# The second half of batch 0: values mixed at full height and regrouped by transfers, keys two rows at a time, queries transposed for both quads

## The chip, the cores and the metric

The kernel runs on one NeuronCore of a Trainium2 chip. Five engines work from their own instruction queues: TensorE (PE, with weight loads shown apart as PEld), VectorE (DVE), ScalarE (ACT), GpSimd (POOL) and SyncE (SP). Instructions of one engine run in program order; engines wait for each other by semaphores. Transfers are issued by SP or POOL (one by ACT) and are carried out by 16 DMA engines. The metric is the device time of one execution in microseconds.

## The reference, cut to what matters

Two stages follow each other: a block-sorted attention and a mixture of four experts. q, k and v are 4 batches x 8 heads x 768 positions x 64; sort_net gives an 8 x 8 matrix per batch and head.

```python
for _ in range(5):                                   # P = sort_net, per batch and head
    P = exp(P - max); P /= rowsum; P /= colsum
k_sorted = einsum('bhij,bhjcd->bhicd', P, k_blocks)  # 8 blocks of 96 positions
v_sorted = einsum('bhij,bhjcd->bhicd', P, v_blocks)
attn = softmax(q_blocks @ k_sorted.T / 8)            # inside each block
x = (attn @ v_sorted)                                # 3072 tokens x 512
p = domain_probs / sum
out = sum_e p[:, e] * (relu(x @ w1[e]) @ w2[e])      # 512 -> 1024 -> 512, 4 experts
```

So each sorted block is a weighted sum of the 8 blocks of its head ("mixing"), and the attention is local to a block.

## The kernel before

**Names.** P = 128, NB = 8 blocks, CP = 16, R = 6, HB = 4 blocks (half of them), VW = 66. A quad (qd) is four heads; sg picks a pair of heads inside it and hh one of the pair. k and v of a quad lie in the tile `arena` with partition = (block j, c) and 6 rows of 64 per partition, so that a block's 96 positions are (c, r). A matmul with the matrix PI0 (built from the sorted weights and an identity mask) mixes the blocks.

**Batch 0 in halves.** Batch 0 has its own path (functions whose names begin with h_), worked in two halves of four output blocks (hf 0 and 1), and each half in two quarters of blocks (qq 0 to 3).

- `h_k` and `h_v` (lines 511 to 515) call `mix_half` (L485): 24 matmuls per quad (L495), each with one row r of one head as 128 x 64 weights and 64 moving columns, the two heads of a pair in the two halves of the output partitions. `mixed` (L503) copies the result from PSUM to `kTs[qd]` or `vT0[qd]`, both with head and dimension on the partitions.
- `h_w` (L517) transposes `vT0` back to position-major by 8 matmuls against the identity (L522), and copies to `vs0s[qd]` (L527), 96 partitions x (block, sg, hh, 66), whose two extra columns hold ones for the softmax sum.
- `h_q` (L264) transposes the queries in `q0` by 24 small matmuls per quad and half (L271) into `qT0[qd]`. q0 holds quad qd on the partitions 64 qd and up.
- `h_s` (L540) makes the scores of one quad and quarter and their exponentials (ACT, L556) in `ETs`; `h_a` (L561) multiplies them with `vs0s` (L567) and normalizes on DVE (L580, L581); `h_x` (L590) transposes into `xTs[0]` (L598, L602).
- `group0` (L666) and `second_layer0` (L708) are expert 0's two layers for batch 0, with matmuls at L679 and L714 and evacuations at L692 (ACT) and L723 (DVE). `own_weights` (L247) makes expert 0's token weights a column per token, by a transpose of `p_0` (6 x 128, f32).

**Order.** The order of all work is the order in which the program emits it; nothing is rearranged. Lines 1365 to 1417 are the first half by hand, with the keys' mixing of the second half (`h_k(0, 1)`, `h_k(1, 1)`) between the groups of the first layer. Then `h_v(0, 1)` and `h_q(0, 1)`, then `second_layer0(0, next_stages)`, which calls `next_stages` in the middle and at the end of each of its three column groups; every call takes the next entry of the list `later` (L1439). After six calls `chunk_first` for the experts 1 and 2 goes on taking entries (L790 matmuls, L796 evacuations on DVE).

**Buffers.** PSUM tiles come in turn from two pools of two buffers, `psA` (attention, function `psa`) and `psM` (experts, `psm`); a new tile waits until the one two before it has been read.

**Transfers.** SP issues, in order: two small loads at the start; then one step of `spread_weights` (L229): the store of the first token weights to DRAM (L241), the load of `p_0` (L242), the spread of four experts' token weights over 128 partitions, 512 KB (L217), and the store of the remaining token weights (L244); then `load_p_one` (L226), 128 KB, needed at L796 near 58.75 us. POOL issues the loads of q, k, v and of all expert weights (`load_w1` L131, `load_w2` L138).

Of the kernel before, what the change touches and what calls it, by code (L numbers as in the profile page):

```python
# [9 lines left out]
F32 = mybir.dt.float32  # L10
F16 = mybir.dt.float16
# [6 lines left out]
def kernel(  # L18
# [11 lines left out]
    nc = tc.nc  # L30
# [36 lines left out]
    def psa(shape, dtype, name):  # L67
        state["n"] += 1
        return psA.tile(shape, dtype, tag="ps", name=name)
# [53 lines left out]
    def head(b, nm, h):  # L123
        return natural[(b, nm, h // 4)][:, h % 4, :, :]
# [6 lines left out]
    def load_w1(e, parts=1):  # L131
        n = NKC // parts
        for i in range(parts):
            nc.gpsimd.dma_start(
                w1sb[e][:, ds(i * n, n)], moe_w1[e].rearrange("(kc p) f -> p kc f", p=P)[:, ds(i * n, n)]
            )
# [20 lines left out]
    def p_part(at, n):  # L157
        return Tt[2].rearrange("p a f x -> p (a f x)")[:, ds(2 * at, 2 * n)].bitcast(F32)
# [47 lines left out]

    p_dram = dramp.tile([E, N], F32, name="p_dram")
    p_sb = const.tile([P, R, 1], F32, name="p_sb")
    p_0 = p_part(2 * E * NT + NT, P)[0:R]
    ident6 = p_part(2 * E * NT + NT + P, R)[0:R]  # L210
    S_P = S // NT

    pbs = {}
# [15 lines left out]
    def spread_weights():  # L229

        nc.vector.tensor_reduce(p_den, p_in, AX.X, ALU.add)
        yield
        nc.vector.tensor_scalar(out=p_den, in0=p_den, scalar1=1e-9, scalar2=None, op0=ALU.add)
        yield
        nc.vector.reciprocal(p_den, p_den)
        yield
        nc.vector.tensor_tensor(
            p_out.rearrange("p e t -> p t e"), p_in, p_den.broadcast_to([P, NT, E]), ALU.mult
        )
        p_rows = p_dram.rearrange("e (p t) -> p e t", t=NT)  # L240
        nc.sync.dma_start(p_rows[0:S_P], p_out[0:S_P])  # L241
        nc.sync.dma_start(p_0, p_dram[0, 0:S].rearrange("(t p) -> t p", p=P))  # L242
        pbs[(0, 0)] = load_p(0, 0)
        nc.sync.dma_start(p_rows[S_P:P], p_out[S_P:P])  # L244
        yield

    def own_weights(ps):  # L247

        nc.tensor.transpose(ps, p_0, ident6)
        nc.vector.tensor_copy(p_sb.rearrange("p t o -> p (t o)"), ps)  # L250


# [11 lines left out]
    def h_q(qd, hf, copy):  # L264

        ps = psa([P, 2, R, 64], F16, f"ps_q_{qd}_{hf}")
        rows = ds(64 * qd, 64)
        for sg in range(2):
            for r in range(R):
                for hh in range(2):  # L270
                    nc.tensor.transpose(  # L271
                        ps[ds(D * hh, D), sg, r, :], q0[rows, hf, 2 * sg + hh, r, :], ident[rows, rows]
                    )
        copy(qT0[qd][:, :, hf], ps[:])
# [4 lines left out]
    sn16 = const.tile([GH, NB, NB, CP], F16, name="sn16")  # L279
    warm(84)  # L280
    p_steps = spread_weights()
    nc.gpsimd.tensor_copy(ident6, ident[0:R, 0:R])
    for it in range(5):
        nc.scalar.activation(sn[:], sn[:], AF.Exp, bias=0.0, scale=1.0)
        if it == 4:
# [199 lines left out]
    def mix_half(nm, qd, hf, pool, warm_up=0):  # L485

        ps = pool([P, 1024], F32, f"ps_m{nm}_{qd}_{hf}")
        keep_warm(ps[:, 0:P], warm_up)
        tails[(nm, qd, hf)] = ps[:, 2 * R * 64:1024].bitcast(F16).rearrange("p (n x) -> p n x", n=2)
        ps = ps[:, 0:2 * R * 64].rearrange("p (s r x) -> p s r x", s=2, r=R)  # L490
        for sg in range(2):
            for r in range(R):
                for hh in range(2):
                    h = 4 * qd + 2 * sg + hh
                    nc.tensor.matmul(  # L495
                        ps[ds(D * hh, D), sg, r, :],
                        head(0, nm, h)[:, r, :],
                        PI0[hf][:, h, :, :].rearrange("p i c -> p (i c)"),
                        start=True, stop=True,
                    )  # L500
        return ps

    def mixed(nm, qd, ps, i0, n, copy):  # L503

        dst = kTs[qd][:, 0:S] if nm == "k" else vT0[qd]
        copy(
            dst.rearrange("p (i x c) -> p x i c", i=HB, c=CP)[:, :, ds(i0, n)],
            ps.rearrange("p s r (i c) -> p (s r) i c", c=CP)[:, :, ds(i0, n)],
        )

    def h_k(qd, hf, copy, pool=psa):
        mixed("k", qd, mix_half("k", qd, hf, pool), 0, HB, copy)

    def h_v(qd, hf, copy, pool=psa):
        mixed("v", qd, mix_half("v", qd, hf, pool), 0, HB, copy)

    def h_w(qd, copy, i0=0, n=HB, at=None):  # L517

# [888 lines left out]
    h_x(1, act, [0], ps_s01)  # L1407
    evacuate00()
    group0(0, 1, 1, [2, 3])
    h_a(1, 1, ps_s11)  # L1410
    h_k(0, 1, act)
    group0(1, 1, 0, [0, 1])
    h_x(1, vec, [1], ps_s11)
    group0(1, 1, 1, [0, 1])
    h_k(1, 1, vec)
    group0(1, 1, 0, [2, 3])
    group0(1, 1, 1, [2, 3])


    load_w1(1)  # L1420
    load_w1(2)
    nc.gpsimd.memset(vo[:, :, :, ds(D, 2)], 1.0)
    nc.gpsimd.tensor_copy(
        maskv.rearrange("p (c i) -> p c i", i=NB),
        eye16.rearrange("p (c o) -> p c o", o=1).broadcast_to([P, CP, NB]),
# [2 lines left out]
    def builds(b):  # L1428
# [8 lines left out]
    builds(1)  # L1437

    later = [  # L1439
        [(h_q, 1, 1, vec)],  # L1440
        [(h_v, 1, 1, act)],
        [(h_s, 0, 2), (h_w, 1, vec)],
        [(h_w, 0, vec), (h_s, 1, 2)],
        [(h_a, 0, 2)],
        [(h_s, 0, 3), (h_a, 1, 2)],
        [(h_s, 1, 3), (h_a, 0, 3)],
# [6 lines left out]
            for f, *args in later.pop(0):  # L1453
                f(*args)

    h_v(0, 1, act)
    h_q(0, 1, vec)
    second_layer0(0, next_stages)
    load_queries(1, range(2))
    for qd in range(2):  # L1460
# [75 lines left out]
```

## Time and profile before

| what | us |
|---|---|
| median of 3 runs (359.15 to 359.76) | 359.17 |
| profiled execution: span from first to last instruction | 357.8 |
| median less span: what lies around the instructions | 1.4 |
| PE busy | 351.6 |
| DVE busy | 276.2 |
| ACT busy | 170.6 |
| POOL busy | 133.6 |
| first product of h_a with the second half, quad 0 / quad 1 | 35.91 / 37.39 |
| first L790 matmul | 37.65 |

The profiled execution is known by its span; its own total is not given apart from the runs. A line of the timeline has the start in us, the length in us, the engine, the source line, the operation, what it writes and reads, the shape, how often (x), and in brackets idle time before it with what ended it. Matmuls are pipelined, so the start-to-start distance of two pieces is their price, and the stated length includes the way through the array.

### The profile page before, as it was taken

What the parts mean: (1) busy time and instruction counts of PE and PEld (TensorE: products, weight loads), DVE (VectorE), ACT (ScalarE), POOL (GpSimd) and SP (SyncE); (2) the same over time, 40 slices, a digit from 0 to 9 for tenths busy, and PEclk for the clock granted to TensorE, in tenths of its full rate; (3) what the DMA queues carried; (4) which work ended last, traced back from release to release, by engine and by line L of the source; (5) the groups of instructions that cost most, each with busy time, mean ns of one, the idle gap of its engine ahead of it and who ended that gap; (6) DMA issues with size and microseconds to landing.
All of it is one profiled execution on the core that took longest, in us unless ns stands there. A gap on an engine that the chain in (4) does not pass through costs nothing.

```text
span 357.8 us, 9498 instructions
## 1 busy us (share of the span) xinstructions
PE 351.6 (98%) x3949; PEld 306.3 (86%) x3949; DVE 276.2 (77%) x552; ACT 170.6 (48%) x303; POOL 133.6 (37%) x149
## 2 busy tenths in 40 slices
PE   8899999999999999999999999999999999999996
PEld 8686867888888888888899988888888888888886
DVE  5754797869889587868978988896678886588963
ACT  2554240442434535367947258830288611688201
POOL 8864010375122222000535318840058800188400
PEclk9999999999999999999999999999999999999999
DMA  8999999999999999935996420005200015100011
GB/s 114 207 205 228 216 210 198 209 163 165 201 154 160 188 152 170 194 74 73 168 201 90 102 78 0 2 2 108 102 29 2 3 39 138 61 0 2 2 73 46
DMA packets 72022, 40.51 MB, mean 113 GB/s; under 512 B 40614, under 2 KB 66732, under 8 KB 71980
## 3 DMA queue, kind: packets, MB, share of 16 engines
q0 software_dynamic: 36576, 19.93, 41.9%
q1 hardware_dynamic: 35260, 19.92, 28.5%
q8 instruction: 31, 0.51, 0.6%
q14 instruction: 11, 0.09, 0.1%
q10 hardware_dynamic: 144, 0.07, 0.1%
HBM read 42.13 MB, written 6.34 MB: 135 GB/s over the span
## 4 chain that ended last, share of the span: by engine, by line
PE 95%; DVE 2%; ACT 1%; DMA 0%; issue 0%; DVEq 0%
PE ps_h L790 18%; PE ps_Q L1264 18%; PE ps_p L774 12%; PE ps_X L1121 10%; PE ps_Z L1121 7%; PE ps_Q L1121 7%; PE ps_Z L1264 6%; PE ps_h L679 3%; PE ps_o L714 3%; PE ps_p L830 3%; PE ps_a L453 2%; PE ps_s L418 2%; PE ps_k L399 1%; PE ps_v L365 1%; PE ps_a L567 1%; PE ps_mk L495 1%
## 5 line engine op out<-in xcount | busy, mean ns | idle before, releaser
L790 PE MATMUL ps_h<-xT,w 128*128 128x256 f16 x576 | 67.5, 273 | 0.0
L790 PEld LDWEIGHTS <-w 128*128 128x128 f16 x576 | 55.2, 98 | 7.2
L796 DVE SCALAR_TENSOR_TENSOR Hb<-ps_h,pb 128x1024 f16<-128x1024 f32 x34 | 41.5, 1223 | 17.2 <-PE ps_h L790 15.8
L1121 PEld LDWEIGHTS <-w 128*128 128x128 f16 x480 | 43.6, 98 | 4.8
L1134 POOL TENSOR_TENSOR arena<-tmp,pb 128x512 f16<-128x512 f32 x12 | 15.2, 1275 | 65.7 <-PE ps_Z L1121 49.8
L1264 PEld LDWEIGHTS <-Hb 128*128 128x128 f16 x320 | 31.1, 98 | 3.5
L1133 ACT ACTIVATE tmp<-tmp 128x512 f32<-128x512 f32 x46 | 29.0, 632 | 3.9 <-DVE tmp L1171 3.9
L1264 PEld LDWEIGHTS <-Sb 128*128 128x128 f16 x304 | 28.3, 98 | 3.0
L1121 PEld LDWEIGHTS <-arena 128*128 128x128 f16 x312 | 27.7, 98 | 2.9
L425 ACT ACTIVATE ET<-ps_s 96x768 f16<-96x768 f32 x24 | 18.0, 802 | 25.1 <-PE ps_s L418 24.8
L121 POOL DMA_DIRECT2D arena<-in_q_dram x24 | 19.9, 838 | 25.5 <-DMA q_ring<-arena 25.2
L408 ACT CAST kT<-ps_k 64x384 f16<-64x384 f32 x48 | 22.7, 473 | 13.3 <-PE ps_k L399 12.3
L1121 PE MATMUL ps_X<-ET,arena 128*128 128x256 f16 x168 | 25.2, 272 | 0.0
L1264 PE MATMUL ps_Q<-w,Hb 128*128 128x256 f16 x192 | 24.6, 273 | 0.0
L774 PEld LDWEIGHTS <-Hb 128*128 128x128 f16 x232 | 21.8, 98 | 3.0
L1127 DVE SCALAR_TENSOR_TENSOR Hb<-ps_X,pb 128x512 f16<-128x512 f32 x27 | 18.7, 691 | 7.0 <-PE ps_X L1121 7.0
L1141 ACT COPY ps_X<-ps_Z 128x512 f32<-128x512 f32 x27 | 15.4, 571 | 17.8 <-PE ps_Z L1121 17.8
L1121 PE MATMUL ps_Z<-xT,w 128*128 128x256 f16 (+1 forms) x176 | 22.5, 258 | 0.0
L760 DVE TENSOR_TENSOR Sb<-Hb 128x512 f16<-128x512 f16 x33 | 20.6, 647 | 0.0
L1148 ACT COPY tmp<-ps_X 128x512 f32<-128x512 f32 x26 | 15.2, 585 | 9.2 <-PE ps_X L1121 6.6
L1127 DVE SCALAR_TENSOR_TENSOR Hb<-ps_Z,pb 128x512 f16<-128x512 f32 x27 | 18.4, 682 | 1.3 <-PE ps_Z L1121 1.3
L1171 DVE TENSOR_TENSOR tmp<-ps_Q,tmp 128x512 f32<-128x512 f32 x26 | 17.8, 683 | 0.8 <-PE ps_Q L1121 0.8
(266 smaller groups left out, 741.6 us busy)
## 6 DMA issues: line engine op xcount, KB each, us to landing
w<-in_moe_w_dram POOLq DMA_DIRECT2D x6, 1024.0 KB, 27.9
pb<-p_dram SPq DMA_DIRECT2D x9, 512.0 KB, 7.0
arena<-in_k_dram POOLq DMA_DIRECT2D x8, 384.0 KB, 9.3
arena<-in_v_dram POOLq DMA_DIRECT2D x8, 384.0 KB, 7.5
vs<-arena SPq DMA_DIRECT2D x36, 66.0 KB, 4.9
arena<-in_q_dram POOLq DMA_DIRECT2D x24, 96.0 KB, 7.5
out_dram<-ob SPq DMA_DIRECT2D x9, 256.0 KB, 2.0
w<-in_moe_w_dram POOLq DMA_DIRECT2D x4, 512.0 KB, 12.5
```

What stands on the lines that cost most here:

```text
L121: nc.gpsimd.dma_start(t[:, h // 2, :, h % 2, :], q[b, h].rearrange("(t p) d -> p t d", p=P))
L408: nc.scalar.copy(kT[ds(D * hh, D), r], pk[ds(D * r, D), hh].rearrange("p a (i c) -> p a i c", c=CP),)
L425: nc.scalar.activation(ETs[2 * (pr % 2) + hh][:, 0:S].rearrange("c (a x) -> c a x", a=2), pss[hh][0:BLK, :, 0:HS], AF.Exp, bias=0.0, scale ...
L760: tt(sm[0], blk(0, 1), blk(1, 1), ALU.add)
L774: nc.tensor.matmul(ps, lhs(e, f), Ts[e][rhs][:, f, :], start=(first and e == es[0] and f == 0), stop=(done and e == es[-1] and f == KH - 1 ...
L790: nc.tensor.matmul(ps[:, f, :], w1sb[e][:, kc, ds((4 * g + f) * P, P)], xT[:, kc, ds(2 * c * P, 2 * P)], start=(kc == 0), stop=(kc == NKC ...
L796: nc.vector.scalar_tensor_tensor(out=Hb[:, homes.get(e, e), ds(4 * g, 4), :], in0=ps[:], scalar=0.0, op0=ALU.max, in1=weights(e).broadcast ...
L1121: nc.tensor.matmul(dst[:, ds(f * cols, cols)], a[lhs][:, k, ds((f0 + f) * P, P)], t[rhs][:, k, :], start=(first and f == 0 and k == 0), st ...
L1127: nc.vector.scalar_tensor_tensor(out=home(i, j), in0=src.rearrange("p (f x) -> p f x", f=m), scalar=0.0, op0=ALU.max, in1=weight(j).broadc ...
L1133: nc.scalar.activation(src, src, AF.Relu, bias=0.0, scale=1.0)
L1171: tt(t12, Q, u2, ALU.add)
L1264: nc.tensor.matmul(ps, lhs(e, f), Ts[e][rhs][:, f, part], start=(first and e == 0 and f == 0), stop=(e == E - 1 and f == KH - 1), skip_gro ...
```

## The change

The first half (hf 0) stays as it is. For the second half:

- **Values.** `h_v` and `h_w` go. `half_v(qd, sg)` uses PI0 as weights (128 x 64) and all six rows of a head as 384 moving columns, one matmul per head, so the result has (block, c) on 64 partitions. ACT copies it to `vo1s[qd]`, and after the second pair SP issues four transfers per quad, one per block, which move 16 partitions x 6 rows to 96 partitions of `vs0s[qd][:, i]`.
- **Keys.** `h_k` becomes `half_k`: two rows of a head as 128 x 128 weights, PI0 as 64 moving columns, 12 matmuls per quad; four copies per quad put it into `kTs[qd]`, two by ACT and two by DVE.
- **Queries.** `pair_q` copies the second half of q0 on DVE so that two heads lie side by side; `half_q` transposes both quads by 12 full transposes; two DVE copies fill `qT0`.
- **Token weights.** `p_0` becomes 128 x 128, zero but for six rows, and `own_weights` a plain f32 matmul.
- **Order.** The four half_v stand among the groups of the first layer where h_k was; half_k(0) precedes `second_layer0`; half_q and half_k(1) are the first two entries of `later`. The loads of w1 of the experts 1 and 2 are emitted earlier, with a fill for each vo1.

```diff
-    p_0 = p_part(2 * E * NT + NT, P)[0:R]
-    ident6 = p_part(2 * E * NT + NT + P, R)[0:R]
+    p_0 = p_part(2 * E * NT + NT, P)
+    ident6 = p_part(2 * E * NT + NT + P, R)
+    nc.gpsimd.memset(p_0, 0.0)
...
-        nc.sync.dma_start(p_0, p_dram[0, 0:S].rearrange("(t p) -> t p", p=P))
+        nc.sync.dma_start(p_0[0:R], p_dram[0, 0:S].rearrange("(t p) -> t p", p=P))
...
-        nc.tensor.transpose(ps, p_0, ident6)
+        nc.tensor.matmul(ps, p_0, ident6, start=True, stop=True)
...
-    nc.gpsimd.tensor_copy(ident6, ident[0:R, 0:R])
+    nc.gpsimd.tensor_copy(ident6, ident[:, 0:R])
...
+    vo1s = [vo, Tt[0].rearrange("p a f x -> p (a f x)")[:, 0:R * 4 * VW].rearrange("p (r h w) -> p r h w", r=R, h=4)]
+
+    def half_v(qd, sg, copy):
+
+        ps = psa([P, 2, 512], F32, f"ps_v0_{qd}_{sg}")[0:CP * HB]
+        for hh in range(2):
+            h = 2 * sg + hh
+            nc.tensor.matmul(
+                ps[:, hh, 0:R * D],
+                PI0[1][:, 4 * qd + h].rearrange("p i c -> p (i c)"),
+                head(0, "v", 4 * qd + h).rearrange("p r d -> p (r d)"),
+                start=True, stop=True,
+            )
+        vo1 = vo1s[qd][0:CP * HB]
+        copy(
+            vo1[:, :, ds(2 * sg, 2), 0:D],
+            ps[:, :, 0:R * D].rearrange("p h (r d) -> p r h d", r=R),
+        )
+        if sg:
+            for i in range(HB):
+                nc.sync.dma_start(
+                    vs0s[qd][:, i].rearrange("x s h w -> x (s h w)"),
+                    vo1[ds(i * CP, CP)].rearrange("c r h w -> c r (h w)"),
+                )
+
+    def half_k(qd, copies):
+
+        ps = psa([P, 2, 512], F32, f"ps_k0_{qd}")
+        pk = ps[:, :, 0:R * 64].rearrange("p h (s a i c) -> p h s a i c", s=2, i=HB, c=CP)
+        for hh in range(2):
+            for sg in range(2):
+                h = 4 * qd + 2 * sg + hh
+                for a in range(R // 2):
+                    nc.tensor.matmul(
+                        ps[:, hh, ds((sg * (R // 2) + a) * 64, 64)],
+                        head(0, "k", h)[:, ds(2 * a, 2), :].rearrange("p r d -> p (r d)"),
+                        PI0[1][:, h, :, :].rearrange("p i c -> p (i c)"),
+                        start=True, stop=True,
+                    )
+        kT = kTs[qd][:, 0:S].rearrange("p (i s c a r) -> p r s a i c", i=HB, s=2, c=CP, r=2)
+        for hh in range(2):
+            for r in range(2):
+                copies[hh](kT[ds(D * hh, D), r], pk[ds(D * r, D), hh])
+
+    q1 = Tt[1].rearrange("p a f x -> p (a f x)")[:, 0:2 * R * P].rearrange("p (s r x) -> p s r x", s=2, r=R)
+
+    def pair_q():
+
+        for sg in range(2):
+            nc.vector.tensor_copy(
+                q1[:, sg].rearrange("p r (h d) -> p r h d", h=2),
+                q0[:, 1, ds(2 * sg, 2)].rearrange("p h r d -> p r h d"),
+            )
+
+    def half_q(copy):
+
+        ps = psa([P, 2, 1024], F16, "ps_q1")
+        for sg in range(2):
+            for r in range(R):
+                nc.tensor.transpose(ps[:, sg, ds(r * P, P)], q1[:, sg, r], ident[:])
+        for qd in range(2):
+            copy(
+                qT0[qd][:, :, 1],
+                ps[:, :, 0:R * P].rearrange("p s (r q x) -> p s r q x", r=R, q=2)[:, :, :, qd],
+            )
...
     group0(0, 1, 1, [2, 3])
+    for vo1 in vo1s:
+        nc.gpsimd.memset(vo1[:, :, :, ds(D, 2)], 1.0)
+    load_w1(1)
+    load_w1(2)
     h_a(1, 1, ps_s11)
-    h_k(0, 1, act)
+    half_v(0, 0, act)
     group0(1, 1, 0, [0, 1])
     h_x(1, vec, [1], ps_s11)
     group0(1, 1, 1, [0, 1])
-    h_k(1, 1, vec)
+    half_v(0, 1, act)
+    pair_q()
     group0(1, 1, 0, [2, 3])
+    half_v(1, 0, act)
     group0(1, 1, 1, [2, 3])
-
-
-    load_w1(1)
-    load_w1(2)
-    nc.gpsimd.memset(vo[:, :, :, ds(D, 2)], 1.0)
+    half_v(1, 1, act)
...
     later = [
-        [(h_q, 1, 1, vec)],
-        [(h_v, 1, 1, act)],
-        [(h_s, 0, 2), (h_w, 1, vec)],
-        [(h_w, 0, vec), (h_s, 1, 2)],
+        [(half_q, vec)],
+        [(half_k, 1, (vec, act))],
+        [(h_s, 0, 2)],
+        [(h_s, 1, 2)],
         [(h_a, 0, 2)],
         [(h_s, 0, 3), (h_a, 1, 2)],
         [(h_s, 1, 3), (h_a, 0, 3)],
...
-    h_v(0, 1, act)
-    h_q(0, 1, vec)
+    half_k(0, (act, vec))
     second_layer0(0, next_stages)
```

## The prediction

> **What bounds the kernel now.** I read the page first: span, busy shares, and the chain that ended last.
>
> ```profile
> span 357.8 us, 9498 instructions
> PE 351.6 (98%) x3949; PEld 306.3 (86%) x3949; DVE 276.2 (77%) x552; ACT 170.6 (48%) x303; POOL 133.6 (37%) x149
> ...
> PE 95%; DVE 2%; ACT 1%; DMA 0%; issue 0%; DVEq 0%
> ```
>
> TensorE is busy for all but 6.2 us and makes up 95% of the chain, so any time it stands still is added to the end, and any matmul time saved is taken off it, unless a wait that follows takes it back. Of the waits of PE the longest two are 1.1 and 1.0 us, both before 12 us; after 28 us none is listed, so later slack can hardly give a delay back.
>
> Next, busy time by stretches: the changed stage runs from about 18 us to 37.65 us, where the first expert's matmuls (L790) begin.
>
> ```profile
> 18.20:28.04 9.84, 9.53 (x193) 8.55 (x190) 5.19 (x12) 5.99 (x10) 7.04 (x9) 1.00 1.24 206
> 28.04:37.65 9.61, 9.61 (x160) 5.64 (x155) 5.33 (x10) 3.71 (x6) 2.92 (x4) 1.00 1.13 229
> ```
>
> Columns after the length: PE, PEld, DVE, ACT, POOL busy, clock, share of the DMA engines, GB/s. PE is full; DVE and ACT have room; the DMA engines are over 1.1 busy, filled by the weight loads that POOL has queued. Then the timeline of PE, for the price of each piece and for when the attention products are wanted:
>
> ```profile
> 27.54 0.57 PE L495 MATMUL ps_mv<-Sb,arena 128*64 128x64 f16 x24
> 28.04 0.56 PE L271 MATMUL ps_q<-ident,T 64*64 64x64 f16 x24
> 28.54 1.04 PE L714 MATMUL ps_o<-w,Hb 128*128 128x512 f16 x4
> ...
> 35.91 0.41 PE L567 MATMUL ps_a<-Sb,ET 96*128 96x65 f16 x8
> ...
> 37.39 0.42 PE L567 MATMUL ps_a<-Sb,ET 96*128 96x65 f16 x8
> ```
>
> The prices are start to start: 24 small matmuls take 0.50. The L567 lines are h_a(0, 2) and h_a(1, 2), the first readers of the second half of the values. Last, the transfers that SP issues in this stretch, and the table of issues in the window 20 to 44 us (median time to landing last):
>
> ```profile
> 20.58 0.34 SPq L241 DMA_DIRECT2D p_dram<-T  x1
> 26.17 0.33 SPq L242 DMA_DIRECT2D T<-p_dram  x1
> 26.55 0.41 SPq L217 DMA_DIRECT2D pb<-p_dram  x1
> 27.00 0.49 SPq L244 DMA_DIRECT2D p_dram<-T  x1
> 27.62 0.53 SPq L226 DMA_DIRECT2D T<-p_dram  x1
> ```
>
> ```profile
> pb<-p_dram SPq DMA_DIRECT2D x1, 512.0 KB, 11.7
> ...
> T<-p_dram SPq DMA_DIRECT2D x1, 128.0 KB, 14.4
> p_dram<-T SPq DMA_DIRECT2D x1, 36.0 KB, 13.9
> ```
>
> The 36 KB of L244 land at 27.0 + 13.9 = 40.9 us, after the 512 KB of L217 (26.55 + 11.7 = 38.3) that were issued ahead of them on the same queue, and L226's 128 KB land after that, at 27.62 + 14.4 = 42.0. What SP issues here comes in order, and late.
>
> **The change part by part.**
>
> *PE, removed.* Four mixings of 24 matmuls (L495) at 0.50, two sets of 24 query transposes (L271) at 0.50, two sets of 8 value transposes (L522) at 0.48 and 0.54 (32.87 to 33.35, 34.22 to 34.76), and three gaps of 0.08 to 0.09 where PE goes from full tiles to half ones (25.53 to 25.61, 27.45 to 27.54, 29.41 to 29.50): 2.0 + 1.0 + 1.0 + 0.3 = 4.3 us.
>
> *PE, added.* half_v: 8 matmuls of 384 columns; two such (L365) take 65.05 to 65.37, so 0.16 each, 1.3. half_k: 24 matmuls with 128-column weights; six such (L399, twice as many columns) take 68.31 to 68.65, 0.057 each, 1.4; with half the columns it could be 0.03 each, 0.7. half_q: 12 transposes at 0.06 (L522), 0.7. own_weights: a full-height f32 matmul in place of the 6-row transpose, which takes 0.15; no row shows one, so 0.15 to 0.6. Sum 3.7 with 0.3 for it, so 0.6 saved, between 0.3 and 1.4.
>
> *PSUM and ACT.* psA has two buffers, and each half_v is emptied by ACT in 0.80 (L371), alternating with the 0.76 that each group evacuation takes. Replaying the order from L692's end at 24.61: the four copies end near 25.4, 26.9, 28.5 and 30.1. half_k(0) would be due at 28.0 but needs the buffer that is free at 28.5: 0.5 lost. half_q is due near 30.1 as the fourth copy ends: 0 to 0.1. Earlier, h_x(1) cannot start before the DVE product that ends at 24.62, and less stands in front of it: 0.15. These holds take 0.7, so h_a(0, 2) would be wanted at 35.91 - 0.6 + 0.7 = 36.0, between 35.2 and 36.4.
>
> *Other engines.* ACT gets 4 x 0.80 + 4 x 0.47 (L408) = 5.1 for 0.82 + 2 x 0.80 = 2.4. DVE gets pair_q (two copies of 768 f16, 0.42 to 0.56 each by L760 and L274), half_q's two at 0.56 and half_k's four at 0.56 (L602 on DVE) = 4.5 for 0.96 + 2 x 0.56 + 2 x 0.68 = 3.4. half_k writes with a step of several elements, which no row shows; if that doubled its copies, 1 us would be added on each engine and could reach PE at h_s. POOL gets small fills: p_0 in front of a wait of 1.22 us (L304), vo1 ahead of the two loads at L134 (some 0.3, with the load queue already full). I put all of this and the PE sum at nothing, because the wait below starts at 36.0 and hides whatever happens before it, up to 6 us.
>
> *The transfers, the added wait.* vs0s of the second half now arrives by eight transfers on SP: four per quad, each 96 pieces of 528 B, 51 KB. In SP's order they stand behind L241, L242, L217 and L244, all issued by one step of spread_weights. SP is free at 27.5, quad 0's values are copied at 26.9, and an issue takes 0.6 (L379), so quad 0 is issued from 27.5 to 29.9 and quad 1, copied at 30.1, from 30.1 to 32.5: long before L244 lands. They then move in order behind it. L226, now behind them, shows the pace: 128 pieces, 128 KB, in 1.1 us. A new transfer is 0.75 of that by pieces (0.83 us) and 0.40 by bytes (0.43); I take 0.65. h_a(0, 2) needs the first two: 40.9 + 1.3 = 42.2 (41.8 to 42.6). h_a(1, 2) needs the sixth: 40.9 + 3.9 = 44.8 (43.5 to 45.9).
>
> On PE, h_a(0, 2) waits from 36.0 to 42.2. Behind it stand in order four L714 (0.87), h_s(0, 3) and h_a(1, 2); these take 1.4 and then wait for 44.8. h_a(1, 2), at 37.39 before, starts at 44.9: 7.5 later (6.2 to 8.6). After it, the order is as before, and h_a(0, 3) and h_a(1, 3) find their data at 43.5 and 46.1, before they are due. L226 lands near 47, and its reader (L796) stood at 58.75. The loads of POOL yield some 2 us to 400 KB; the next values landed at 34.04 + 29.5 = 63.5, wanted at 64.94 plus the delay: covered.
>
> *The clock after the wait.* At its start PE is slow:
>
> ```profile
> 1.06:5.70 4.64, 4.64 (x44) 4.64 (x45) 2.31 (x11) 1.48 (x3) 4.35 (x8) 1.00 0.72 105
> 5.70:8.19 2.49, 2.49 (x44) 2.38 (x41) 1.89 (x11) 0.51 (x2) 2.41 (x5) 1.00 1.18 161
> ```
>
> 44 matmuls of 128 columns take 4.64 us, the next 44 take 2.49, although the clock column says 1.00 for both. No pause in this trace shows whether a stop of 6 us brings that back: between 0 and 4.64 - 2.49 = 2.2 us. I take 0.9: the slow stretch starts at 42.2, 2.6 us of it pass before h_a(1, 2), the remaining 2.0 lose nearly half.
>
> The Trainium skill, "TensorE: Matmul & The Clock Gate" (The HAM clock gate), says PE falls to half rate after an idle window of about 3.4 us and needs about as long to come back; that would make the loss 3.4 / 2 = 1.7 us if all of it fell on needed work.
>
> *Sum.* 7.5 + 0.9 = 8.4 on the span of 357.8 gives 366.2; with the 1.4 by which the median of 359.17 stands over the span, 367.6. Bounds: 6.2 + 0 gives 365.4, 8.6 + 2.2 gives 370.0.
>
> A rule that would have it otherwise: the Trainium skill, "DMA: Bandwidth & Descriptors" (Anatomy of one DMA), fits a transfer issued from GpSimd as about 2.0 us plus bytes over 436 GB/s. By that estimate 51 KB land 2.1 us after issue, nothing waits, and the time stays near 359.3. The row of 36 KB with 13.9 us stands against it here.
>
> **The rivals.**
>
> *The transfers are hidden* (not slower). If landing took the 4.9 us that L379's transfers take in the median of the whole run, the second transfer (issued by 28.7) lands at 33.6 and the sixth (by 31.3) at 36.2, both before they are wanted. It decides while landing stays under about 6 us. Then PE's own sum is left: +0.1, from -0.7 to +0.5, or +1.5 if half_k's copies double, so 358.5 to 360.7. For it: that median, and 5.6 us for L241 in the same loads. Against it: L244 and L226, issued in the same microsecond on the same queue.
>
> *A partial wait.* Landing 9.4 us after issue, the longest of L379: 38.1 and 40.7, h_a(1, 2) 3.4 later, perhaps without the slow clock: 362.6, 361.5 to 364. For it: the queue's packets may not be strictly in order. Against: L226 behind L244 behind L217.
>
> *A longer wait.* If h_a waits for all four transfers of its quad, the eighth counts: two more at 0.65, 1.3 us, so 369, up to 371.3.
>
> **How the numbers follow.** Forecast 0.77; longer wait 0.08; partial wait 0.08; hidden 0.07. The likeliest gives 367.6. The range reaches from 363.5, in the upper part of the partial wait, to 371.3, the top of the longer one; the hidden case and most of the partial one stay outside. A measurement of this kernel tells about 0.2% (0.7 us) from no change. The hidden case splits into faster 0.02, same 0.04, slower 0.01; the rest is slower.
>
> **What would show it.** In the changed profile: PE idle for some 6 us before the first L567-type product of the third quarter, ended by a DMA into vs0s (tile Sb), and about 1 us before the second quad's; transfers from vo with landing times of 11 to 15 us; no matmuls of mix_half or h_q between 23 and 35 us; L790 matmuls just after the wait nearer 0.2 us apart than 0.11. It is wrong if those transfers land within 6 us of issue, if PE shows no wait there, or if a copy by ACT or DVE ends the wait.

## The result, and the profile after

| | us |
|---|---|
| before, median of 4 runs (359.15 to 359.94) | 359.47 |
| after, median of 4 runs (370.23 to 371.15) | 370.78 |
| ratio after / before, 95% interval | 1.0313 (1.0299 to 1.0328) |
| profiled execution of after: time / span | 370.47 / 368.7 |
| forecast, and its range | 367.6 (363.5 to 371.3) |

The kernel became 11.3 us slower. The sign was foreseen and the size nearly so; where the time was lost was not. The page of after, its span, busy times, PE's row of slices with its clock, and the chain that ended last:

```profile
span 368.7 us, 9305 instructions
PE 354.2 (96%) x3834; PEld 305.4 (83%) x3834; DVE 283.2 (77%) x555; ACT 176.7 (48%) x308; POOL 134.0 (36%) x151
...
PE   8795699999999999999999999999999999999996
PEclk9999699999999999999999999999999999999999
...
PE 89%; DMA 3%; DVE 3%; ACT 2%; POOL 1%; issue 1%; ACTq 0%; DVEq 0%; POOLq 0%
```

PE executes 115 fewer matmul instructions, and its idle time has grown from 6.2 to 14.5 us. The loss lies in one place, the fourth and fifth slice (about 28 to 46 us), where PE is at 0.5 to 0.6 and the clock dips too. Comparing the start of the same work further on, PE is 9.9 us behind at 70 us and still 9.9 behind at 157 us; near 181 us 0.4 is added (a wait before an attention product, L454), and about as much in the tail.

What PE waited for, from the list of waits of the whole run (engine, tile and line that waited, releaser; total us, times, longest):

```profile
PE ps_k L551 <- DVE kT L560: 3.9, 1, 3.9
PE ps_s L617 <- ACT kT L560: 3.4, 1, 3.4
```

The next ones on the list are the old ones from the start, 1.2 and 1.1. These two are new, and neither is a transfer: both end with a copy of half_k (L560). The timeline of after shows how that comes about (start, length, engine, line, operation, result and operand, shape, count, idle time before it and what ended it):

```profile
28.37 0.52 PE L551 MATMUL ps_k<-Sb,arena 128*128 128x64 f16 x12
...
29.59 2.89 ACT L560 CAST kT<-ps_k 64x384 f16<-64x384 f32 x2
...
32.51 2.86 DVE L560 CAST kT<-ps_k 64x384 f16<-64x384 f32 x2 [3.28 <-ACT kT L560]
...
35.52 0.51 PE L551 MATMUL ps_k<-Sb,arena 128*128 128x64 f16 x12 [3.95 <-DVE kT L560]
35.86 1.53 PE L781 MATMUL ps_o<-w,Hb 128*128 128x512 f16 x4
37.20 2.85 DVE L560 CAST kT<-ps_k 64x384 f16<-64x384 f32 x2
...
40.16 2.85 ACT L560 CAST kT<-ps_k 64x384 f16<-64x384 f32 x2 [7.68 <-DVE kT L560]
...
43.06 0.50 PE L617 MATMUL ps_s<-Sb,kT 64*128 64x96 f16 x8 [3.42 <-ACT kT L560]
43.49 1.89 PE L781 MATMUL ps_o<-w,Hb 128*128 128x512 f16 x4
45.18 0.65 PE L634 MATMUL ps_a<-Sb,ET 96*128 96x65 f16 x8
...
47.54 1.91 PE L857 MATMUL ps_h<-xT,w 128*128 128x256 f16 x16
```

Two things are to be seen. Each copy takes 1.43 us, where copies of the same size took 0.47 to 0.56. And the two engines, meant to share the four copies of a quad, take turns: DVE begins (32.51) when ACT's two are done (32.48), so a quad's copies last 5.7 us. half_k(1) needs the PSUM buffer of half_k(0) and stands until 35.5. Then the same follows for quad 1, DVE first, and the scores (L617) stand until 43.06. The first matmul of the next experts (L857, L790 in the kernel before) starts at 47.54, against 37.65: 9.9 later. Of that 3.95 + 3.42 = 7.4 are the two waits. The pieces from these scores to the experts take 43.06 to 47.54, 4.5 us. In the kernel before the same pieces took 2.9:

```profile
34.76 0.35 PE L550 MATMUL ps_s<-Sb,kT 64*128 64x96 f16 x8
...
37.65 1.91 PE L790 MATMUL ps_h<-xT,w 128*128 128x256 f16 x16
```

So 1.6 more go to slow matmuls behind the second wait. The windows of after show the clock there (length; busy time and instructions of PE, PEld, DVE, ACT, POOL; clock; DMA share; GB/s):

```profile
44.00:46.00 2.00, 2.00 (x13) 0.95 (x12) 0.14 (x1) 0.54 (x1) 0.00 (x0) 0.50 1.23 213
46.00:48.00 2.00, 2.00 (x25) 1.13 (x24) 1.61 (x4) 0.60 (x1) 0.16 (x1) 0.88 1.21 228
```

A clock of 0.50 after the wait, 0.88 two microseconds on. The remaining 0.9 us are smaller delays ahead of the second wait, above all the group of four at 35.86, behind the first wait: 1.46 instead of 0.87, with a clock of 0.56 from 36 to 38 us.

And the transfers of the values? The table of issues of after, 20 to 60 us (KB each, median us from issue to landing):

```profile
Sb<-arena SPq DMA_DIRECT2D x4, 49.5 KB, 14.2
Sb<-T SPq DMA_DIRECT2D x4, 49.5 KB, 9.0
...
p_dram<-T SPq DMA_DIRECT2D x1, 36.0 KB, 14.3
```

They are as late as forecast: issued from 27.45 on, the second landed at 42.4. But the attention product that reads it (L634) was held until 45.18 by the copies in front of it, so nobody waited for a transfer.

### The profile page after: what moved, and what is told of

Its sections match the earlier page's. It is cut to its first block, busy times and chain, and to the rows that moved or that the text cites. A ratio compares the mean times of both kernels' runs of the same rounds, so it can differ in the third digit from the quotient of the medians.

```text
span 368.7 us, 9305 instructions
## 1 busy us (share of the span) xinstructions
PE 354.2 (96%) x3834; PEld 305.4 (83%) x3834; DVE 283.2 (77%) x555; ACT 176.7 (48%) x308; POOL 134.0 (36%) x151
## 4 chain that ended last, share of the span: by engine, by line
PE 89%; DMA 3%; DVE 3%; ACT 2%; POOL 1%; issue 1%; ACTq 0%; DVEq 0%; POOLq 0%
PE ps_h L857 17%; PE ps_Q L1331 17%; PE ps_p L841 12%; PE ps_X L1188 10%; PE ps_Z L1188 6%; PE ps_Q L1188 6%; PE ps_Z L1331 6%; DMA arena<-in_v_dram 3%; PE ps_p L897 3%; PE ps_h L746 2%; PE ps_o L781 2%; PE ps_a L454 2%; ACT kT L560 2%; DVE kT L560 2%; PE ps_s L419 2%; PE ps_k L400 1%
## 5 line engine op out<-in xcount | busy, mean ns | idle before, releaser
L857 PE MATMUL ps_h<-xT,w 128*128 128x256 f16 x576 | 67.5, 273 | 0.0
L857 PEld LDWEIGHTS <-w 128*128 128x128 f16 x576 | 55.2, 98 | 7.2
```

The costliest lines, as they stand in the source:

```text
L857: nc.tensor.matmul(ps[:, f, :], w1sb[e][:, kc, ds((4 * g + f) * P, P)], xT[:, kc, ds(2 * c * P, 2 * P)], start=(kc == 0), stop=(kc == NKC ...
```

## The experiments

Two causes fitted the rows: the copies of half_k, which the trace names, and the transfers, which the trace shows late but hidden. The first set takes each away, alone and together.

### The transfers taken away

```diff
-        if sg:
-            for i in range(HB):
-                nc.sync.dma_start(
-                    vs0s[qd][:, i].rearrange("x s h w -> x (s h w)"),
-                    vo1[ds(i * CP, CP)].rearrange("c r h w -> c r (h w)"),
-                )
```

> The changed kernel without the eight transfers from vo1s to vs0s; the second half of the values therefore stays that of the first half. Theory A (half_k's copies, 1.4 us each and one after the other, hold PE, and the transfers land behind that): the time stays at 370 to 371.5, and PE still waits about 3.9 us at the second quad's half_k and 3.4 us at its scores. Theory B (the wait for the transfers holds PE, as I forecast): the time falls to 360 to 364.

Measured: 370.43 us (4 runs), ratio 1.0302 (1.0277 to 1.0327). PE's first waits in this kernel (lines are six lower here):

```profile
PE ps_k L545 <- DVE kT L554: 3.9, 1, 3.9
PE ps_s L611 <- ACT kT L554: 3.4, 1, 3.4
```

Same waits, and the same time within the spread of the runs: in the changed kernel the transfers cost nothing that these runs resolve.

### The keys written in neighbouring elements

A copy runs over c innermost. kT holds a block's positions in the order (c, a, r), so the results of neighbouring c lie six elements, 12 bytes, apart. The order (a, r, c) makes runs of 16 neighbours. The change scatters the keys because its transfers lay a block's values down in the order (c, row); in this kernel the keys therefore stand in another order than the values.

```diff
-        kT = kTs[qd][:, 0:S].rearrange("p (i s c a r) -> p r s a i c", i=HB, s=2, c=CP, r=2)
+        kT = kTs[qd][:, 0:S].rearrange("p (i s a r c) -> p r s a i c", i=HB, s=2, c=CP, r=2)
```

> The changed kernel with half_k's copies writing 16 neighbouring elements at a time (order i s a r c), so that the keys of a block stand in another order than the values. Theory A: each copy falls from 1.43 us to about 0.5, the two waits on copies shrink below 1 us each, PE then comes to h_a(0, 2) near 37 and waits there for the transfers until about 42.4, and again until about 45.4: 367 to 369.5 in all. Rival (the copies are the whole loss, the transfers cost nothing): 359.5 to 361.5. Theory B: unchanged, 370 to 371.5.

Measured: 369.89 us (4 runs), 1.0294 (1.0261 to 1.0327); the profiled execution took 369.23 with a span of 367.4. The copies by line and form (total busy us, mean ns; idle time before them):

```profile
L560 DVE CAST kT<-ps_k 64x384 f16<-64x384 f32 x4 | 2.2, 551 | 2.2 <-PE ps_q L577 2.2
...
L560 ACT CAST kT<-ps_k 64x384 f16<-64x384 f32 x4 | 1.9, 477 | 4.2 <-DVE kT L560 4.2
```

They went from 1.43 to 0.48 and 0.55, and yet the kernel gained only 0.9 us. The timeline of PE in this kernel says why:

```profile
35.72 1.04 PE L781 MATMUL ps_o<-w,Hb 128*128 128x512 f16 x4
...
41.46 0.22 PE L634 MATMUL ps_a<-Sb,ET 96*128 96x65 f16 x1 [4.71 <-DMA Sb<-arena]
42.14 0.55 PE L634 MATMUL ps_a<-Sb,ET 96*128 96x65 f16 x7 [0.46 <-DMA Sb<-arena]
...
45.23 0.54 PE L634 MATMUL ps_a<-Sb,ET 96*128 96x65 f16 x7 [0.24 <-DMA Sb<-T]
45.59 2.78 PE L857 MATMUL ps_h<-xT,w 128*128 128x256 f16 x16
```

This is the chain of the forecast. The second transfer releases h_a(0, 2) at 42.14 (forecast 42.2), the sixth h_a(1, 2) at 45.23 (44.8), the first expert starts at 45.59, 7.9 later than before (forecast 7.5; it is 8.3 if both are counted from the first group of the first layer, which began 0.4 earlier here), and its first group runs slowly, as the windows of this kernel show:

```profile
42.14:45.59 3.45, 3.21 (x28) 1.57 (x28) 1.64 (x3) 0.72 (x1) 0.00 (x0) 0.50 1.21 213
45.59:48.30 2.71, 2.71 (x21) 1.93 (x19) 0.89 (x2) 0.09 (x1) 0.74 (x1) 0.67 1.23 224
```

The stretch from 45.59 to 48.30 takes 2.71 us; its work took 1.84 before: 0.87 lost to the clock (0.9 forecast).

### Both taken away

Both edits above in one kernel.

> Both edits together: copies of neighbouring elements and no transfers (keys in another order, values of the first half). Theory A, in which both losses stand in each other's shadow: 359.5 to 362, near the kernel before, since neither wait is left; what stays is the order of the copies on ACT and DVE. If a third cost of some size exists (pair_q's copies of 1.9 us on DVE, PSUM buffers), 363 to 366.

Measured: 360.95 us (10 runs), 1.0042 (1.0029 to 1.0055). PE's waits on the keys' copies in this kernel:

```profile
PE ps_s L611 <- ACT kT L554: 1.3, 1, 1.3
...
PE ps_k L545 <- DVE kT L554: 0.3, 1, 0.3
```

So the two losses stand in each other's shadow, each hidden by the other. By medians: removing the transfers alone gains 0.4, plain copies alone 0.9, both 9.8. And what is left of the change once both are gone is not a gain but 1.6 us of loss. The next experts start at 38.31, 0.66 later than before, although the stage began 0.38 earlier (its first group at 18.81 instead of 19.19). So the stage lasts 1.04 longer, and 1.6 of it are the two waits shown: PE's own work in it is some 0.6 shorter. Another 0.9 is lost near 181 us, where PE waits 0.8 before an attention product (L454). The kernel without the transfers waits 0.9 there and the two-tile kernel below not at all, so no run ties this wait to a part of the change.

### Every second element

The order (a, c, r): neighbouring results 4 bytes apart.

```diff
-        kT = kTs[qd][:, 0:S].rearrange("p (i s a r c) -> p r s a i c", i=HB, s=2, c=CP, r=2)
+        kT = kTs[qd][:, 0:S].rearrange("p (i s a c r) -> p r s a i c", i=HB, s=2, c=CP, r=2)
```

> The changed kernel with half_k's copies writing every second element (order i s a c r, 4 bytes apart) instead of every sixth (12 bytes); the keys of a block are in another order. If any write that is not to neighbouring elements is slow, the copies stay at 1.4 us and the time at 370 to 371.5. If it is the distance, the copies fall towards 0.5 us and the time to 367 to 369.5.

Measured: 369.69 us (one run). The copies by line and form:

```profile
L560 ACT CAST kT<-ps_k 64x384 f16<-64x384 f32 x4 | 2.3, 575 | 4.3 <-DVE kT L560 4.3
L560 DVE CAST kT<-ps_k 64x384 f16<-64x384 f32 x4 | 2.3, 568 | 1.8 <-ACT kT L560 1.8
```

0.57 at 4 bytes, 1.43 at 12 bytes, 0.48 and 0.55 for neighbours: of the steps tried, only the longer one costs much, so it is not a step as such. PE then waits for the transfers, 5.3 us in all, as with neighbours. The Trainium skill, "SBUF — State Buffer" (Door 1: The DMA port swizzle), has a rule that fits: SBUF has lines of 16 bytes, and accesses run at full speed while at least two in a row fall into the same line. Steps of 4 bytes put four into a line, steps of 12 bytes at most two and mostly one. The page gives no price; here it is a factor of 2.6 to 3. The same passage lets 16-bit data stride up to 8 elements for free, and that does not hold here, where 6 elements cost this much. With two step sizes measured, the line as the cause is an argument, not shown.

### Upper keys in a tile of their own

Do the engines take turns because they write one tile? Here the upper half of the keys goes to another SBUF tile. The 12-byte steps stay, the transfers are left out.

```diff
...
-        kT = kTs[qd][:, 0:S].rearrange("p (i s c a r) -> p r s a i c", i=HB, s=2, c=CP, r=2)
         for hh in range(2):
+            kT = (kTs, kUs)[hh][qd][:, 0:S].rearrange("p (i s c a r) -> p r s a i c", i=HB, s=2, c=CP, r=2)
...
```

> The changed kernel without the transfers (values of the first half stay), half_k's scattered copies unchanged at 1.43 us each, but the upper half of the keys in a tile of its own, so that the two engines' copies no longer write the same tile. If ACT and DVE take turns only because the copies name one tile, they now run side by side: the first wait on copies falls from 3.9 to about 1 us, the second from 3.4 to about 1.5, and the time to 362 to 365. If the turns have another reason (both read one PSUM tile), they stay and the time is 370 to 371.

Measured: 369.31 us (4 runs), 1.0265 (1.0242 to 1.0288). The timeline:

```profile
29.45 2.88 ACT L557 CAST kT<-ps_k 64x384 f16<-64x384 f32 x2
...
32.37 2.85 DVE L557 CAST T<-ps_k 64x384 f16<-64x384 f32 x2 [3.45 <-ACT kT L557]
```

The turns stay, with two destinations. What the copies still share is the PSUM tile that both read (different halves of it), and in the program as built DVE's first copy waits on the semaphore that ACT raises after its second. So the order is the built program's, between two readers of one PSUM tile. (The 1.1 us by which this kernel lies below the one without transfers are not of this stage: it lacks the wait near 181 us.) Whether a PSUM tile for each engine would undo it was not tried and stays open.

### The transfers on ACT's queue

If SP's queue is what makes them late, another queue must help. From the kernel with plain copies, the eight transfers are issued by ACT, behind half_k(0), and no longer by SP in half_v.

```diff
...
     half_k(0, (act, vec))
+    for qd in range(2):
+        for i in range(HB):
+            nc.scalar.dma_start(
+                vs0s[qd][:, i].rearrange("x s h w -> x (s h w)"),
+                vo1s[qd][ds(i * CP, CP)].rearrange("c r h w -> c r (h w)"),
+            )
     second_layer0(0, next_stages)
```

> The kernel of k_plain (copies of neighbouring elements, keys in another order), with the eight transfers issued by ACT after half_k(0) instead of by SP behind the 512 KB and 36 KB. If the place in SP's queue is what makes them late, they land some 5 to 6 us after issue, h_a waits at most 1 us, and the time is 360.5 to 363. If the DMA engines being full is what makes them late, whatever the queue, they land 12 us or more after issue and the time stays at 368 to 371.

Measured: 372.75 us (4 runs), 1.0355 (1.0330 to 1.0380), the slowest of all. The table of issues of this kernel, then its timeline:

```profile
Sb<-arena ACTq DMA_DIRECT2D x4, 49.5 KB, 8.3
Sb<-T ACTq DMA_DIRECT2D x4, 49.5 KB, 5.5
```

```profile
33.70 10.90 ACTq L1522 DMA_DIRECT2D Sb<-T  x4
44.70 0.95 ACT L554 CAST kT<-ps_k 64x384 f16<-64x384 f32 x2 [12.24 <-DMA T<-p_dram]
...
45.71 0.50 PE L611 MATMUL ps_s<-Sb,kT 64*128 64x96 f16 x8 [9.32 <-ACT kT L554]
```

The place in the queue does matter: quad 0's transfers land 8.3 us after issue (median), not 14, and before the 36 KB that SP had issued ahead of them (42.92). But the four issues of quad 1 took 10.9 us, and ACT can do nothing else meanwhile, so half_k(1)'s copies start at 44.70 and PE stands for 9.3. (1.9 us of this kernel's lateness arose before the changed stage: its first group starts at 21.06 in the profiled execution.)

The trace tells what held the issues. Every transfer of SP and ACT raises one of eight semaphores when it lands, used in turn for both engines, and an issue whose turn meets a transfer still under way waits for it. ACT's last three issues start at 40.16, 42.94 and 44.03, each right after the landing of the transfer that had their semaphore before: the 512 KB (40.14), the 36 KB (42.92) and the 128 KB (44.01). In after SP's seventh and eighth issue waited in the same way, for the 512 KB (landed 37.16, issue 37.23) and the 36 KB (41.12, 41.19). So the hold is an order in the built program, and no limit of a queue is needed to explain it; the expected gain failed on it.

### The 512 KB and the 36 KB issued earlier

This kernel and the one with dummy matmuls are compared with a base of their own: plain copies of half_k, and in place of the 24 transposing transfers of the later batches plain transfers of the same tiles. Its changed stage runs as with plain copies.

> The base of the next two: the kernel of k_plain (half_k's copies write 16 neighbouring elements, keys in another order than the values), with the 24 transposing transfers of the batches 1 to 3 replaced by plain copies of the same tiles, so that these batches compute with untransposed queries and tokens. The first plain copy comes after 61 us, so the changed stage should look as in k_plain: waits at h_a(0, 2) until about 42.1 us and at h_a(1, 2), first group of the first expert 45.6 to 48.3 us. The total is a base of its own, between 362 and 371, since plain copies may land sooner or later than transposing ones.

Measured: 368.42 us (4 runs), 1.0233 (1.0206 to 1.0259), with the second transfer releasing PE at 42.22 and the first expert at 45.67 (42.14 and 45.59 in the kernel it stands for).

Now the step of spread_weights that issues the 512 KB, the 36 KB and their kin is moved some 4 us earlier:

```diff
     mixed("v", 0, mv0, 2, 2, vec)
+    next(p_steps)
     mk1 = mix_half("k", 1, 0, psm)
...
     h_a(1, 0, ps_a10)
-    next(p_steps)
     group0(0, 1, 0, [0, 1])
```

> k_plain_c (plain copies for the transposing transfers), with the fourth step of spread_weights, which issues the store of token weights, the 512 KB spread and the 36 KB store, about 4 us earlier. If the eight transfers are late because of what stands ahead of them on SP's queue, the 512 KB are through by 31 us, the eight land some 6 to 8 us after issue, h_a waits less than 1 us, the first expert starts near 38.5 us instead of 45.6, and the total falls by 7.5 to 9.5 us against k_plain_c. If the load of the DMA engines is the reason, whatever stands ahead, nothing changes by more than 1 us.

Measured: 367.65 us (4 runs), 1.0216 (1.0187 to 1.0245), 0.8 less than the base, with overlapping runs (366.76 to 368.54, base 367.43 to 368.67), and far from the 7.5 to 9.5 that had been expected if the place in the queue were all; by its size alone it fits the other expectation, that the load of the DMA engines decides. The first expert starts 1.2 earlier (44.45), although this execution's stage began 0.55 later. SP issued the two at 22.55 and 23.00 instead of 26.16 and 26.60; the 512 KB landed 4.0 us earlier (33.80), the 36 KB only 2.1 (38.52), and h_a(0, 2) was released at 41.21, 1.0 earlier. The transfers by queue (packets, MB, share of the engines), for the 4.75 us from 33.75 to 38.5 of this kernel:

```profile
q0 software_dynamic: 448, 0.89, 99.6%
q1 hardware_dynamic: 448, 0.11, 18.0%
```

and for the 4 us from 37.2 to 41.2 of the kernel with plain copies:

```profile
q0 software_dynamic: 611, 0.68, 98.0%
q1 hardware_dynamic: 616, 0.16, 29.8%
```

SP's queue (hardware) and POOL's (software, the weight loads) move equal numbers of packets. SP's moves 94 packets per us beside packets of 2 KB (0.89 MB in 448) and about 150 beside packets of 1.1 KB, although its own are smaller in both windows (0.25 KB on average). So, piece for piece, the 36 KB (384 pieces of 96 B) ahead of the values cost as much queue as the 512 KB (512 of 1 KB). Issued earlier, they pass beside larger weight packets, and most of the head start is lost. By these windows the lever is the number of packets ahead in the queue, and what the other queue carries meanwhile, more than the moment of issue; no run changed these alone.

### Dummy matmuls against the slow clock

95 matmuls into an unused PSUM half directly ahead of h_a(0, 2), so that PE is not idle while the transfers come.

```diff
-        [(h_a, 0, 2)],
+        [(lambda: warm_wait(),), (h_a, 0, 2)],
```

> k_plain_c with 95 matmuls of 128 columns that nobody reads, placed before h_a(0, 2), where PE waits for the transfers (5.2 us at full clock). If the slow clock after the wait costs time of its own, PE comes out of the wait at full clock, the first group of the first expert takes 1.84 us instead of 2.71, and the total falls by about 0.9 us against k_plain_c. If the slow clock costs nothing, no change; if the dummies outlast the wait, a rise.

Measured: 367.97 us (5 runs, 367.69 to 371.71), 1.0232 (1.0203 to 1.0261); the base had 368.42, so a difference of 0.45 that these runs don't resolve. The mean granted clock of four of the five executions rose to 0.999 or 1.000, from 0.986 to 0.991. The profiled one is the longest of the five and doesn't show what the others won: there h_a(0, 2) starts at 42.09 without a wait, and h_a(1, 2) waits 0.95 + 1.50 for the transfers of quad 1; behind that the clock reads 0.52 (46.5 to 50 us), so that the stage gains nothing. The clock's price is therefore known from the windows with plain copies (0.87), not from this kernel.

### The rest of the change

Keys and queries put into the kernel before, without transfers: half_k in plain order with one engine for a quad's four copies, and the queries transposed straight from q0 by 24 transposes, without pair_q. The values stay as before.

```diff
-    h_k(0, 1, act)
+    half_k(0, act)
...
-    h_k(1, 1, vec)
+    half_k(1, vec)
...
-        [(h_q, 1, 1, vec)],
+        [],
...
     h_v(0, 1, act)
-    h_q(0, 1, vec)
+    half_q(vec)
```

> The kernel before, with two parts of the change in another form, and nothing of its values or transfers: half_k at the places of the two h_k, two rows at a time, copied in the order of before (16 neighbouring elements), all four copies of a quad on one engine; and the second half's queries of both quads transposed by 24 transposes of full height straight from q0, without pair_q. PE should need 2 x 0.36 for 2 x 0.59 of h_k and about 0.75 for 2 x 0.59 of h_q: 0.9 us less, 358.3 to 358.9, if the longer copies (1.9 and 2.2 us for 0.8 and 0.96) stay hidden; if they hold a PSUM buffer too long, 359 to 361.

Measured: 361.36 us (12 runs, 359.82 to 363.65), 1.0046 (1.0022 to 1.0069): not faster, rather 0.5% slower. The timeline:

```profile
26.39 2.31 DVE L549 CAST kT<-ps_k 64x384 f16<-64x384 f32 x4 [0.60 <-PE ps_k L540]
...
28.85 0.86 PE L523 MATMUL ps_q<-ident,T 128*64 128x128 f16 x24 [0.68 <-DVE kT L549]
...
38.15 1.91 PE L824 MATMUL ps_h<-xT,w 128*128 128x256 f16 x16
```

Four copies by one engine hold the buffer for 2.3 us and PE stands 0.68 for it; the experts start at 38.15, 0.5 later than before (0.36 if both are counted from the first group of the first layer). The larger part of the profiled execution's loss, 1.2 us, comes near 98 us, where PE waits for an evacuation that itself waits for a transfer of token weights (pb); no run ties that to the copies. Fewer matmuls, more copies: in its stage this part loses too, by the one wait.

The queries alone, in the kernel before with plain transfers for the transposing ones (and without the change's other parts):

> The kernel before (with the same plain copies for the transposing transfers), with one part of the change in another form: the second half's queries of both quads transposed by 24 full-height transposes straight from q0, at the place of the first h_q. To be read in the stage alone: PE should need 0.79 us (as in keys_queries) for 2 x 0.59, so the first expert's first matmul starts 18.1 to 18.2 us after the first L679 matmul instead of 18.46 (19.19 to 37.65). If the two DVE copies in a row hold a PSUM buffer, 18.4 or more.

Measured: 360.37 us (one run). The kernel before was not run with these plain transfers, so the total has nothing to be compared with. Its stage, from the same group of the first layer to the next experts (20.62 to 38.57, 17.95), is 0.5 shorter than before (19.19 to 37.65, 18.46), somewhat more than expected, in one execution of each. This is the one part that shortened its stage.

### POOL's work moved away from pair_q

pair_q's two copies (L567) took 3.8 us together in after, although 0.42 to 0.56 each had been set for them: the first 3.54, the second 0.35. POOL runs four products of 1.04 us (L339, L347) beside them. In the kernel without transfers and with plain copies, these are emitted later:

```diff
-    builds(1)
-
     later = [
...
             load_natural(1, nm, qd)
+    builds(1)
     chunk_first(0, 0, [1, 2], 1, next_stages)
```

> The kernel of k_plain_no_moves (no transfers, keys in another order) with POOL's four builds of 1.04 us each emitted after the loads of the next batch, so that they no longer run beside pair_q. If POOL's work beside them is what stretches the two copies of pair_q to 1.4 to 1.9 us, they fall to 0.3 to 0.6 us each; if it is the copies' own pattern, they stay above 1.4. The time in either case within 1 us of 361.0, since nobody waits for them.

Measured: 364.30 us (one run), 3.4 more than without the move. The timeline:

```profile
25.07 0.62 DVE L561 COPY T<-T 128x768 f16<-128x768 f16 x2
...
51.40 0.69 DVE L806 TENSOR_TENSOR w<-w 128x1024 f16<-128x1024 f16 x1
52.12 4.65 DVE L806 TENSOR_TENSOR T<-w 128x1024 f16<-128x1024 f16 x1
52.16 1.06 POOL L347 TENSOR_TENSOR arena<-maskv,Rs 128x512 f16<-128x512 f16 x1
...
55.18 1.04 POOL L339 TENSOR_TENSOR arena<-maskk,Rs 128x512 f16<-128x512 f16 x1
```

Away from POOL's products the two copies take 0.35 each, 0.62 together, instead of 2.8 together (2.52 and 0.35), so POOL's work was what stretched the first. But now a sum of weights on DVE, 0.69 elsewhere, takes 4.65, until POOL's four are done, and PE waits 3.0 us for an evacuation queued behind it. The expectation that the move would be nearly free missed: the clash moved to where someone waits for it. The Trainium skill, "SBUF — State Buffer" (SBUF: two separate sides), says that DVE, in operations such as one with two inputs in SBUF, and GpSimd share a pair of ports, and that whichever starts first holds it for the whole instruction while the other is blocked. The hold agrees with that, but not its length: DVE was kept out for four instructions in a row (52.16 to 56.22), not for one of 1.05 us.

## Why the prediction was right or wrong

**The step that failed** is half_k's copies: "if that doubled its copies, 1 us would be added on each engine and could reach PE at h_s", and with it "I put all of this and the PE sum at nothing, because the wait below starts at 36.0 and hides whatever happens before it, up to 6 us." The copies were not doubled but 2.6 to 3 times as long, and ACT and DVE did not work side by side: one quad's copies take 5.7 us in a row, two quads' with a chain of PSUM buffer and DVE order between them. That holds PE 7.4 us, more than the 6 us of cover (and h_a(0, 2) until 45.18, when its transfers had landed at 42.4), so the copies hide the transfers and not the other way round. The text named the test itself: wrong "if a copy by ACT or DVE ends the wait". One did. The prediction added up the busy time of each engine. For two engines that empty one PSUM tile one after the other the sum along that chain was wanted, and for the write with a step an upper end beyond a doubling.

**The transfers** were right in mechanism and size, but in after they cost nothing. With the copies made plain, the wait that was forecast appears: releases at 42.14 and 45.23 for 42.2 and 44.8, the next expert 7.9 later for 7.5. That the result lies only 3.2 us above the forecast is luck: the two losses are about equal (370.43 without the transfers, 369.89 without the slow copies), and the one that was forecast did not occur in after. One part of its working was too simple: that the values stand behind the 36 KB "in order" and move at the pace of L226. The order holds, but the pace goes with the packets of POOL's queue, as the two windows beside the earlier issue show.

**The clock.** 0.9 was taken for it, and 0.87 is what the windows with plain copies give. In after it costs 1.6 behind the second wait. The Trainium skill, "TensorE: Matmul & The Clock Gate" (The HAM clock gate), has half rate after an idle window of about 3.4 us; the 0.50 after 3.4 and 4.7 us of idle time agree. In the kernel with dummies a wait of 0.95 + 1.50 us was enough for a clock of 0.52, less than that window. The estimate of 1.7 worked out from it for the whole loss is near the 1.6 of after, where nothing was left to wait for; with plain copies it would have been too much, since part of the slow time fell into waiting for quad 1.

**PE's own sum** (0.6 saved, 0.7 lost to holds) is right in its first half: in the kernel with neither loss PE's work in the stage is some 0.6 shorter. Two of its prices were off and about cancel: half_v's matmuls took 0.22 each instead of 0.16, half_k's 0.03 instead of 0.057. The hold of 0.5 foreseen at half_k(0) did not come (it starts at 28.01, the copy it needs ended at 27.95); in its place stand 1.6 us of waits on half_k's copies, so that the stage is 1.0 longer and not 0.1.

**pair_q's copies** were set at 0.42 to 0.56 each, and the first took 3.54, since POOL's products run beside it. No wait of PE on them is listed, so "nothing" was right for PE.

**The frame.** The forecast added 1.4 for what lies around the span. In every run where both are known it is 1.8 (370.47 and 368.7; 359.31 and 357.5): the 1.4 set the span of one execution against the median of others. That is 0.4 of the 3.2 by which the forecast is short. A further 0.9 us, near 181 us and in the tail, was in no step of it.

**Rivals.** None was this one. "Hidden" and "partial" supposed that the transfers land within about 6 or 9.4 us, and the first ones took 14; the "longer wait" gives the time nearly (369), with a mechanism that didn't happen: with plain copies PE was let go by the second and sixth transfer, not by the fourth and eighth.

## What to carry to other kernels

A cost that is put at nothing because a longer wait covers it needs its upper bound compared with that cover, and where two engines share the emptying of one PSUM tile the safe bound is their sum in a row, not the larger of the two. If a measured loss equals the forecast, look which wait carries it: two losses of equal size in the same place hide each other, and only a kernel without both shows what either is worth. Before fewer matmuls are bought with copies or transfers, count the copies per PSUM buffer and the packets ahead in the queue; here the keys and queries without any transfer lost 0.4 us in their stage as well. And where an issue is held, look which semaphore it waits for before a queue is blamed.

## What the runs showed of the hardware that was not expected

- Writing 64x384 results from PSUM to f16 in SBUF costs 0.48 (ACT) and 0.55 (DVE) us for runs of 16 neighbours, 0.57 on both at steps of 4 bytes, and 1.43 and 1.42 at steps of 12 bytes.
- DVE operations on f16 in SBUF that met POOL's row of products of 1.04 us were held to the end of the row: 0.69 became 4.65, and a copy of 0.35 became 2.52 and 3.54.
- SP's and POOL's queues moved equal numbers of packets (448 and 448, 616 and 611), which fits a queue of small pieces that is paced by the size of the other's pieces.
- An issue that waits for the semaphore of an earlier transfer holds its whole engine: 10.9 us on ACT for four issues. The eight semaphores used in turn are the built program's.
